# Padding ahead of the first fetch, two rows to a packet, and the first conversions spread over a mixture-of-experts stage

## The chip, the cores and the metric

The kernel runs on one core of one Trainium2 chip. The metric is device time in microseconds, the median of the runs shown. Beside these runs there is one profiled execution, whose trace is read below. Engines are named as the profile names them: PE (matmul), PEld (weight load), DVE, ACT, POOL, and SP, which issues nearly all DMAs; SPq is SP's instruction queue.

## The reference, cut to what matters

Three layers follow each other: a retention-like attention, a mixture of eight experts with sticky routing, and a Fourier mix with a two-layer channel network. Only the second is touched by the change:

```python
for b in range(B):                      # 4 sequences
    prev_e = -1
    for s in range(S):                  # 576 tokens each
        fresh_e = argmax(logits[b, s])
        e = fresh_e if s == 0 or local_gate[b, s] < 0.5 or prev_e < 0 else prev_e
        prev_e = e
        h = maximum(x[b, s] @ w1[e], 0)         # 512 -> 1024
        out[b, s] = p[e] * (h @ w2[e])          # 1024 -> 512
```

## The kernel before, in words

**Rows by expert.** At the end of the attention stage each token's row (512 values as a high and a low fp16 part, then its position and its gate: 1056 fp16, 2112 bytes) is scattered by POOL into a DRAM tensor `xs`, sorted by expert. The last six scatters go out just before the expert stage. Each expert gets a fixed number of rows (`CAPS`); what the routing doesn't fill is overwritten with zero rows: `pad(e)` (L1047) writes `CAPS[e] - 128` rows from an SBUF tile of zeros, `z`, 288 of them (608,256 bytes, 594 KB) for expert 1 and 160 or 192 for the others. Where they begin is a value that `tally` (L2019) computes on DVE and SP loads (`start(e)`). `fetch(e)` (L1012) then reads the expert's rows through two or one transposing DMAs into `xt`, and the positions and gates into `mt`. `fetch(0)` reads fixed places and waits for all scatters (`rows_in.before`); `fetch(1)` reads rows that `pad(1)` may have written, and waits for that. `apart` lifts the order between fetches and paddings of different experts; `Rows.add` lifts it between scatters. Neither lifts it between a padding and a scatter.

**Weights.** An expert's weights are eight pieces of 128x1024 fp32 (512 KB), 0 to 3 of w1 and 4 to 7 of w2. Each is sized (`absmax`, ACT L234), and for each four pieces a power of two is found: `peak` (DVE L250 to L255, makes `diag`), `spread` (one PE matmul L260 and a DVE reduction L261), `scale` (DVE L266, L269). Then `split` makes the high part (ACT L276) and the low part (DVE L281).

**Order.** The program's order on each engine is fixed by hand, an engine's instructions run in that order. A first batch of 256 rows of expert 0 (`weights(0)`, two tiles) begins in the attention stage. Then, for e = 0 to 7, a hidden stage of eight steps f (12 matmuls each into one PSUM bank out of four, then `relu`: ACT L826 and DVE L828, the latter frees the bank), and an output stage, a tile of 128 rows at a time (24 matmuls L840, ACT L852, a POOL scatter L854). `halves` (L931) deals other work to slots of these stages by numbers in `SLOTS`; stage n = 2e is the hidden stage of expert e, n = 2e + 1 its output stage. For expert 0 the work is written out in `moe` itself: `parts` splits expert 1's pieces 0 to 3, `sizes` sizes pieces 6 and 7 and begins the conversions.

**Conversions.** `Doubles` converts the channel network's weights, given as 64-bit doubles, to fp32 in 16 pieces, of which 14 go beside the experts: `load` (1 MB, tile `raw`, two buffers), `first` (DVE L294 to L298), `second` (DVE L303, L306), `absmax` (ACT), `store` (DMA).

The order on DVE after expert 0's hidden stage is `first(0)`, `peak` of expert 1's second half, `second(0)`, `first(1)`, `second(1)`, and then the reduction and scale of that second half, whose `spread` matmul PE has after step f = 0 of expert 1. On SP it is the weight loads 0 to 7 of expert 1, `fetch(0)`, `pad(1)`, `fetch(1)`, the loads of `raw` 0 and 1, and then weights of expert 2.

Of the kernel before, what the change touches and what calls it, by code (L numbers as in the profile page):

```python
# [10 lines left out]
FP16 = mybir.dt.float16  # L11
BF16 = mybir.dt.bfloat16
I32 = mybir.dt.int32
# [6 lines left out]
B, H, S, D = 4, 8, 576, 64  # L20
# [19 lines left out]
XW = 1056  # L40
NOPOS = 1 << 20
# [11 lines left out]
DONE = 14  # L53
# [774 lines left out]
    nc.vector.scalar_tensor_tensor(out=l[:, f, :], in0=ps, scalar=0.0, in1=h[:, f, :], op0=ALU.max, op1=ALU.subtract)  # L828


def outputs(nc, ps, q, x2, rows_out, w, hid, mt, fs, t, n, amid=None):

    h, l = w.dst
    k = 128 // min(128, n - 128 * t)
    r, d = 128 // k, 512 // k
    for f in range(8):
        for i, (m, x) in enumerate(((h, 0), (h, 1), (l, 0))):
            for j in range(k):
                c = 512 * (f % 2) + d * j
                nc.tensor.matmul(  # L840
                    out=ps[r * j : r * j + r, 0:d],
                    lhsT=hid[x][:, f, 128 * t : 128 * t + r],
                    rhs=m[:, 4 + f // 2, c : c + d],
                    start=(f == 0 and i == 0),
                    stop=(f == 7 and i == 2),
                )
        if f == 3 and amid:
            amid()

    def leave():  # L850
        y = q()[:, 0:d]
        nc.scalar.activation(out=y, in_=ps[:, 0:d], func=ACTF.Copy, scale=fs)  # L852
        rows_out.add(
            nc.gpsimd.indirect_dma_start(  # L854
                out=x2[:, :].rearrange("t (k d) -> (t k) d", k=k),
                out_offset=bass.IndirectOffsetOnAxis(ap=mt, axis=0),
                in_=y,
                in_offset=None,
                bounds_check=k * NT - 1,
                oob_is_err=False,  # L860
            )
        )

    return leave


class Late:
# [22 lines left out]
    def outputs(self, bank):  # L890
# [13 lines left out]
        second=0,  # L904
        spread=-1,
        split=(0.1, 1.1, 2.1, 3.1),
        raw=1.2,
        store=1.3,
        fetch=1.4,
# [7 lines left out]
        first=(0, 4.2),  # L917
        factors=0.2,
        split=(0.5, 0.6, 1.5, 2.7),
        second=2.8,  # L920
        load=(2, 3, 4, 5),
        size=(3.1, 4.1, 4.6, 5.2),
        raw=5.5,
        store=5.6,
# [6 lines left out]
def halves(weights, conv, n, slots, others=()):  # L931


    jobs = []

    def at(k, f, *a):
        jobs.append((k, len(jobs), partial(f, *a)))

    def matrix(m):
        return (weights(m // 2), m % 2) if m // 2 <= E else (None, 0)  # L940

    S = SLOTS[n % 2]
    if n <= DONE:
        at(S["own"], conv.absmax, n - 1)
    w, i = matrix(n + 1)
    if not (w.one and i):
        if n % 2 == 0:
            at(S["spread"], w.spread, i)
        at(S["spread"], w.scale, i)
    for p in range(4 if not w.one else EARLY_C1):  # L950
        at(S["split"][p], w.split, 4 * i + p)
    w, i = matrix(n + 2)
    if not w.one:
        for p in range(4):
            at(S["size"][p], w.absmax, 4 * i + p)
    if n % 2 or n == 2:
        for m, k in ((n + 3, "load"), (n + 4, "ahead"))[: 1 + n % 2]:
            w, i = matrix(m)
            if w and not (w.one and i):
                for p in range(4):  # L960
                    at(S[k][p], w.load, 4 * i + p)
    for k, f in others:
        at(S[k], *f)

    S = {**S, "first": (4, 0), "second": 5, "store": 5.1, "raw": 5.2} if n == 2 else S
    if n < DONE:
        if n % 2 or n == 2:
            at(S["first"][0], conv.first, n)
        at(S["second"], conv.second, n)
        at(S["store"], conv.store, n)  # L970
        if n + 2 < DONE:
            at(S["raw"], conv.load, n + 2)
        if n % 2 and n + 1 < DONE:
            at(S["first"][1], conv.first, n + 1)
    w, i = matrix(n + 2)
    if not (w.one and i):
        at(S["peak"], w.peak, i)
    todo = [[] for _ in range(slots)]
    for k, _, f in sorted(jobs, key=lambda x: x[:2]):
        todo[int(max(k, 0) * slots / 8)].append(f)  # L980
    return todo


def moe(octx, tc, nc, A, xs, x2, rows_in, rows_out, pieces, weights, who, conv, low, start, beyond, z, hid0, mt0, wst, small):
    ctx = ExitStack()
    pool = lambda **k: ctx.enter_context(tc.tile_pool(reuse_waits="tile", **k))
# [60 lines left out]
    def pad(e):  # L1047
        m = CAPS[e] - ZERO
        i = nc.sync.dma_start(
            out=xs[bass.ds(start(e), m), :].bitcast(I32).rearrange("(t p) c -> p t c", p=32),  # L1050
            in_=z[0:32].bitcast(I32).unsqueeze(1).to_broadcast([32, m // 32, XW // 2]),
        )
        apart(e, i)

# [9 lines left out]

        return fs, fill

    def out(w, hid, mt, fs, t, n, do, amid=None):
        y = lambda: wk.tile([128, 512], FP32, tag="y", name="y", bufs=3)
        ps = p2.tile([128, 512], FP32, tag="ps2", name="ps2")
        leave = outputs(nc, ps, y, x2, rows_out, w, hid, mt[:, t, 0:1], fs[:, t : t + 1], t, n, amid)  # L1070
        for job in do:
            job()
        leave()
# [3 lines left out]
    w1 = weights(1)  # L1077
    n = CAPS[8]
    pieces.more = more
    for p in range(4, 8):  # L1080
        w1.load(p)
    fetch(0)
    pad(1)
    fetch(1)
    conv.load(0)
    conv.load(1)
# [6 lines left out]
    def sizes():  # L1093
        for p in range(6, 8):
            w1.absmax(p)
        conv.first(0)
        w1.peak(1)
        conv.second(0)
        conv.store(0)
        conv.load(2)  # L1100
        conv.absmax(0)
        conv.first(1)
        conv.second(1)
        conv.store(1)
        conv.load(3)

    fs, fill = factors(weights(0), mt0, 2)
    fill()
    w1.peak(0)
    for t in range(2):  # L1110
        out(weights(0), hid0, mt0, fs, t, n, (parts,) if t else (), partial(w1.spread, 0) if t else None)

    v = weights(2)
    first = [[] for _ in range(8)]
    for p in range(4, 6):
        first[0].append(partial(w1.absmax, p))
    first[7].append(beyond)
    for f, p in zip((2, 3, 4, 5), range(4)):
        first[f].append(partial(v.load, p))
    for e in range(E):  # L1120
        w, n = weights(e), CAPS[e] if e < E - 1 else HEAD
        if e == E - 1:
            pieces.more = None
        xt, mt = X.pop(e)
        tiles = (n + 127) // 128

        todo = halves(weights, conv, 2 * e, 8, [("fetch", (fetch, e + 1))] if e + 1 < E else ()) if e else first
        hid = wk.tile([128, 2, 8, n], FP16, tag="hid", name="hid", padded_shape=[128, 2, 8, CAP])
        hid = [hid[:, x] for x in range(2)]
        for f in range(8):  # L1130
            if e == 0 and f % 4 == 0:
                four = [bank()[:, 0:n] for _ in range(4)]
                for part in (0, 2, 1):
                    for g in range(4):
                        products(nc, four[g], *w.dst, xt, f + g, (part,))
            if e == 0:
                ps = four[f % 4]
            else:
                ps = bank()[:, 0:n]
                products(nc, ps, *w.dst, xt, f)  # L1140
            for do in todo[f]:
                do()
            if f == 4 and e + 2 < E:
                pad(e + 2)
            for _ in relu(nc, ps, hid, f):
                pass
        fs, fill = factors(w, mt, tiles + (end.n + 127) // 128, small) if e == E - 1 else factors(w, mt, tiles)
        if e == E - 1:
            end.fs = fs

        def sides(mt=mt, tiles=tiles, n=n, e=e):
            for i, m in ((n // 128, n % 128), (tiles + end.n // 128, end.n % 128 if e == E - 1 else 0)):
                if m:

                    to, k = mt[:, i, 0:1], 128 // m
                    nc.vector.tensor_scalar(out=to, in0=to, scalar1=float(k), scalar2=side[k], op0=ALU.mult, op1=ALU.add)

        late = 0 < e < E - 1
        if not late:
            fill()  # L1160
            sides()
        if e == E - 1:
            mx.close()
            yield
        todo = halves(weights, conv, 2 * e + 1, tiles, [("factors", (f,)) for f in (fill, sides) if late]) if e else [[sizes]]
        for t in range(tiles):

            amid = partial(weights(e + 1).spread, 0, lambda: bank()[:, 0:128]) if e and t == 0 else None
            out(w, hid, mt, fs, t, n, todo[t], amid)
# [988 lines left out]
def fused_kernel(tc, A, out, stop=None):  # L2158
    nc = tc.nc
    with ExitStack() as ctx:  # L2160
# [5 lines left out]
        with tc.manual_schedule():  # L2166
# [39 lines left out]
            keep = ctx.enter_context(tc.tile_pool(name="keep", bufs=1))  # L2206
            fill = ExitStack()

            def zeros(pool):

                z = pool.tile([128, XW], FP16, name="z")
                nc.gpsimd.memset(z, 0.0)
                nc.gpsimd.memset(z[:, 1024:1026].bitcast(I32), NOPOS)
                return z

            z = zeros(fill.enter_context(tc.tile_pool(name="zp", bufs=1)))
# [64 lines left out]
            c2x = ExitStack()  # L2281
            cv = c2x.enter_context(tc.tile_pool(name="cv", bufs=1, reuse_waits="tile"))
            conv = Doubles(nc, cv, jobs)
            z = zeros(cv)
            steps = moe(ctx, tc, nc, A, xs, x2, rows_in, rows_out, pieces, weights, who, conv, low, start, beyond, z, hid0, mt0, wst, small)
            next(steps)
            for t, n in zip(tables, ("f_cs", "f_sn", "f_cd", "f_sd")):
# [53 lines left out]
```

## Time and profile before

| | |
|---|---|
| median of 3 runs | 803.86 us (801.23 to 806.83) |
| the profiled execution | 806.09 us, span of its trace 804.3 us |
| mean granted TensorE clock | 0.983 |
| PE busy | 738.5 us, 92% of the span |
| DVE busy | 590.8 us, 73% |
| ACT busy | 412.2 us, 51% |
| expert 0's first batch, output | PE from 124.8 us |
| expert 0's other rows, hidden and output | 135.2 to 150.5 us |
| expert 1, hidden and output | 150.5 to 193.1 us |
| expert 2 begins | 193.2 us |

The span leaves 1.8 us of the execution outside the trace. Busy shares are means over the whole kernel; what a stage waits for is read in rows of that stage.

### The profile page before, as it was taken

The page shows a single profiled execution, that of the slowest core. Times are in us where ns is not written, and L with a number is a line of the kernel's source. Part 1 is how long each engine was busy: PE and PEld are TensorE (multiplying, and loading weights), DVE is VectorE, ACT ScalarE, POOL GpSimd, SP SyncE. Part 2 cuts the span into 40 slices and gives each one's busy share as a digit, 9 for nine tenths or more (in the row PEclk, how much of TensorE's full clock was granted, in tenths as well). Part 3 has the DMA queues.
Part 4 walks back from the last instruction along what each step waited for, and adds up shares of the span by engine and source line. Part 5 has one row for each costly group of instructions (what it writes and reads, how often), then busy time and mean ns, then how long its engine had stood idle before and what let it go on. Part 6 is the DMA issues. An engine that isn't in the chain of part 4 may idle for free. (4 is left out here: it accounts for less than half of the span.)

```text
span 804.3 us, 17230 instructions
## 1 busy us (share of the span) xinstructions
PE 738.5 (92%) x6571; PEld 550.7 (68%) x6571; DVE 590.8 (73%) x1432; ACT 412.2 (51%) x829; POOL 129.3 (16%) x225
## 2 busy tenths in 40 slices
PE   8888898889999998889989998979899999999996
PEld 5777785545656555557635546868788888888885
DVE  3678886588889988857797984968968495737362
ACT  1356657278888797835728533515523361414140
POOL 3566443002102201113000111010010101010101
PEclk9999999899999999999999998999999999999999
DMA  9998348899999999850528266610370016110000
GB/s 292 360 317 297 118 139 277 274 318 379 261 338 324 259 314 326 271 174 29 167 93 313 93 197 170 189 58 2 106 206 2 27 53 172 53 40 15 27 2 27
DMA packets 91930, 142.29 MB, mean 177 GB/s; under 512 B 48116, under 2 KB 49017, under 8 KB 90814
## 3 DMA queue, kind: packets, MB, share of 16 engines
q1 hardware_dynamic: 87246, 126.78, 50.1%
q0 software_dynamic: 4592, 14.31, 4.7%
q8 instruction: 54, 0.88, 0.4%
q14 instruction: 38, 0.31, 0.1%
HBM read 97.55 MB, written 35.12 MB: 165 GB/s over the span
## 5 line engine op out<-in xcount | busy, mean ns | idle before, releaser
L1637 PE MATMUL g<-gxt,wh 128*128 128x256 f16 (+1 forms) x992 | 145.0, 287 | 4.5 <-DMA gxt<-un 4.3
L1951 PEld LDWEIGHTS <-hd 128*128 128x128 f16 x1176 | 114.9, 98 | 27.1 <-issue 7.6
L1637 PEld LDWEIGHTS <-wh 128*128 128x128 f16 x1056 | 103.9, 99 | 30.9 <-issue 8.4
L281 DVE SCALAR_TENSOR_TENSOR wl<-wst,ws,wh 128x1024 f16<-128x1024 f32 (+1 forms) x82 | 100.5, 1253 | 10.3 <-ACT wh L276 10.1
L276 ACT ACTIVATE wh<-wst,ws 128x1024 f16<-128x1024 f32 x80 | 89.1, 1140 | 24.6 <-DVE ws L269 24.6
L810 PE MATMUL ps<-xt,wh 128*128 128x320 f16 (+4 forms) x544 | 79.1, 284 | 11.1 <-DVE hid L828 7.6
L810 PEld LDWEIGHTS <-wh 128*128 128x128 f16 x640 | 57.6, 101 | 42.0 <-issue 24.4
L840 PE MATMUL ps<-wh,hid 128*128 128x512 f16 (+2 forms) x528 | 84.6, 302 | 0.2 <-ACT hid L826 0.2
L1951 PE MATMUL g<-wh,hd 128*128 128x256 f16 x448 | 79.7, 276 | 3.8 <-DVE u L1980 2.0
L1811 POOL DMA_INDIRECT out<-u,orow x18 | 19.3, 1075 | 394.1 <-DVE u L1980 296.9
L1637 PE MATMUL g<-gxt,wl 128*128 128x256 f16 (+1 forms) x496 | 81.0, 287 | 0.0
L1922 DVE SCALAR_TENSOR_TENSOR s<-g,r 128x256 f32<-128x256 f32 x168 | 53.3, 374 | 34.3 <-ACT hd L1916 33.6
L840 PEld LDWEIGHTS <-hid 128*128 128x128 f16 (+2 forms) x792 | 46.5, 100 | 42.9 <-issue 3.3
L234 ACT ACTIVATE wh<-wst 128x1024 bf16<-128x1024 f32 x66 | 69.3, 1050 | 6.4 <-DVE wst L306 4.1
L1980 DVE SCALAR_TENSOR_TENSOR u<-g,ffs,u 128x256 f32<-128x256 f32 (+1 forms) x63 | 34.1, 568 | 50.5 <-PE g L1951 49.8
L1915 ACT ACTIVATE r<-g 128x256 f32<-128x256 f32 x56 | 21.2, 378 | 95.8 <-PE g L1637 89.7
L1895 ACT ACTIVATE hd<-s 128x640 f16<-128x640 f32 x56 | 41.3, 737 | 47.1 <-DVE s L1922 47.1
L1951 PE MATMUL g<-e,hd 128*128 128x256 f16 x504 | 59.9, 273 | 5.2 <-DVE u L1980 4.2
L854 POOL DMA_INDIRECT x<-y,mt x25 | 32.2, 1287 | 198.8 <-ACT y L852 174.9
L1951 PE MATMUL g<-wl,hd 128*128 128x256 f16 x224 | 61.7, 276 | 0.0
L1637 PEld LDWEIGHTS <-wl 128*128 128x128 f16 x528 | 52.3, 99 | 12.3 <-issue 1.1
L840 PE MATMUL ps<-wl,hid 128*128 128x512 f16 (+2 forms) x264 | 56.3, 301 | 0.0
(302 smaller groups left out, 1293.9 us busy)
## 6 DMA issues: line engine op xcount, KB each, us to landing
wst<-in_moe_w SPq DMA_DIRECT2D x64, 512.0 KB
raw<-in_ch SPq DMA_DIRECT2D x14, 1024.0 KB
qk<-in_qkv SPq DMA_DIRECT2D x18, 512.0 KB
vk<-in_qkv SPq DMA_DIRECT2D x16, 512.0 KB
pair<-ch SPq DMA_DIRECT2D x32, 256.0 KB
ch<-d SPq DMA_DIRECT2D x14, 512.0 KB
wst<-ch SPq DMA_DIRECT2D x14, 512.0 KB
u<-u SPq DMA_DIRECT2D x9, 512.0 KB
```

The source lines that it names most:

```text
L234: self.nc.scalar.activation(out=x, in_=t, func=ACTF.Abs, accum_out=self.am[:, j : j + 1])
L276: self.nc.scalar.activation(out=self.dst[0][:, j, :], in_=self.pieces[j], func=ACTF.Copy, scale=self.by(j))
L281: self.nc.vector.scalar_tensor_tensor(out=l[:, j, c], in0=self.pieces[j][:, c], scalar=self.by(j), in1=h[:, j, c], op0=ALU.mult, op1=ALU.s ...
L810: nc.tensor.matmul(out=ps, lhsT=m[:, k, 128 * f : 128 * f + 128], rhs=xt[:, x + k, :], start=(k == 0 and i == 0), stop=(k == 3 and i == last),
L840: nc.tensor.matmul(out=ps[r * j : r * j + r, 0:d], lhsT=hid[x][:, f, 128 * t : 128 * t + r], rhs=m[:, 4 + f // 2, c : c + d], start=(f == ...
L854: nc.gpsimd.indirect_dma_start(out=x2[:, :].rearrange("t (k d) -> (t k) d", k=k), out_offset=bass.IndirectOffsetOnAxis(ap=mt, axis=0), in_ ...
L1637: nc.tensor.matmul(out=ps, lhsT=m[:, k + 4 * (f // 8), 128 * (f % 8) : 128 * (f % 8) + 128], rhs=xt[x][:, k, :], start=(k == 0 and i == 0) ...
L1895: nc.scalar.activation(out=hd[:, 0, 2:7], in_=s, func=ACTF.Copy, scale=C2 / 2)
L1915: nc.scalar.activation(out=r, in_=p[:, 1:3], func=ACTF.Relu)
L1922: V.scalar_tensor_tensor(out=d, in0=x, scalar=0.0, in1=y, op0=ALU.max, op1=op)
L1951: nc.tensor.matmul(out=ps, lhsT=hid[k][:, y, x, :], rhs=E[w][m][k], start=(k == 0 and m == y == 0), stop=(k == 7 and y == 1),)
L1980: V.scalar_tensor_tensor(out=y, in0=p, scalar=fs[:, c : c + 1], in1=y, op0=ALU.mult, op1=ALU.add)
```

## The change

1. `pad(1)` goes from behind `fetch(0)` to between the loads of pieces 6 and 7 of expert 1.
2. A padding writes two rows to a packet: `z` holds two rows per partition, and 16 partitions are read instead of 32. The memset that fills `z` is twice as wide, with two small ones behind it instead of one.
3. The `spread` of expert 1's first half comes after step 0 instead of step 3 of the first batch's second tile.
4. In expert 0's hidden stage the sizing of pieces 4 and 5 goes from step 0 to steps 4 and 5, and steps 4 to 7 run as those of other experts instead of in a batch of four.
5. `second(1)`, `store(1)` and the load of `raw` 3 go from `sizes` to slot 3 of expert 1's hidden stage, the conversion's `absmax(1)` to slot 4; `first(2)` from slot 4 to slot 5. `second(2)`, `store(2)` and the load of `raw` 4 go to the start of expert 1's output stage, `absmax(2)` to its second tile. `fetch(2)` goes from slot 1 to slot 3.

```diff
-        if f == 3 and amid:
+        if f == at and amid:
...
     S = SLOTS[n % 2]
-    if n <= DONE:
+    if n == 2:
+        S = {**S, "fetch": 3.6}
+    if 3 < n <= DONE:
         at(S["own"], conv.absmax, n - 1)
...
-    S = {**S, "first": (4, 0), "second": 5, "store": 5.1, "raw": 5.2} if n == 2 else S
-    if n < DONE:
-        if n % 2 or n == 2:
+    def ends(k, j):
+        at(k, conv.second, j)
+        at(k, conv.store, j)
+        if j + 2 < DONE:
+            at(k, conv.load, j + 2)
+
+    if n == 2:
+        ends(3, 1)
+        at(4.5, conv.absmax, 1)
+        at(5, conv.first, 2)
+    elif n < DONE:
+        if n == 3:
+            ends(0, 2)
+            at(2, conv.absmax, 2)
+        if n % 2:
             at(S["first"][0], conv.first, n)
...
-            out=xs[bass.ds(start(e), m), :].bitcast(I32).rearrange("(t p) c -> p t c", p=32),
-            in_=z[0:32].bitcast(I32).unsqueeze(1).to_broadcast([32, m // 32, XW // 2]),
+            out=xs[bass.ds(start(e), m), :].bitcast(I32).rearrange("(t p a) c -> p t (a c)", p=16, a=2),
+            in_=z[0:16].bitcast(I32).unsqueeze(1).to_broadcast([16, m // 32, XW]),
...
-    for p in range(4, 8):
+    for p in range(4, 7):
         w1.load(p)
+    pad(1)
+    w1.load(7)
     fetch(0)
-    pad(1)
     fetch(1)
...
         conv.first(1)
-        conv.second(1)
-        conv.store(1)
-        conv.load(3)
...
-        out(weights(0), hid0, mt0, fs, t, n, (parts,) if t else (), partial(w1.spread, 0) if t else None)
+        out(weights(0), hid0, mt0, fs, t, n, (parts,) if t else (), partial(w1.spread, 0) if t else None, 0)
...
-        first[0].append(partial(w1.absmax, p))
+        first[p].append(partial(w1.absmax, p))
...
-            if e == 0 and f % 4 == 0:
+            if e == 0 and f == 0:
...
-            def zeros(pool):
+            def zeros(pool, rows=1):
-                z = pool.tile([128, XW], FP16, name="z")
+                z = pool.tile([128, rows * XW], FP16, name="z")
                 nc.gpsimd.memset(z, 0.0)
-                nc.gpsimd.memset(z[:, 1024:1026].bitcast(I32), NOPOS)
+                for r in range(rows):
+                    nc.gpsimd.memset(z[:, r * XW + 1024 : r * XW + 1026].bitcast(I32), NOPOS)
...
-            z = zeros(cv)
+            z = zeros(cv, 2)
```

## Rows read from the trace of the kernel before

**Rows 1.** Waits of PE, 120 to 380 us: total us, times, longest.

```profile
PE peak L260 <- DVE diag L255: 9.3, 6, 3.1
PE ps L810 <- DVE hid L828: 7.6, 5, 3.1
```

**Rows 2.** Timeline of PE: start, us, engine, line, operation, count, [idle before <- releaser].

```profile
141.06 2.79 PE L810 MATMUL ps<-xt,wh 128*128 128x128 f16 x32 [3.00 <-DVE hid L828]
...
155.95 0.27 PE L260 MATMUL peak<-diag,onesb 128*128 128x128 bf16 x1 [3.14 <-DVE diag L255]
...
167.05 0.86 PE L810 MATMUL ps<-xt,wh 128*128 128x416 f16 x4 [3.06 <-DVE hid L828]
...
178.68 0.22 PE L260 MATMUL ps<-diag,onesb 128*128 128x128 bf16 x1 [0.44 <-DVE diag L255]
```

**Rows 3.** Timeline of DVE, expert 0's output stage to expert 2.

```profile
153.17 0.69 DVE L294 TENSOR_SCALAR d<-raw 128x1024 int32<-128x1024 int32 x1 [5.24 <-DMA raw<-in_ch]
...
155.61 0.29 DVE L255 TENSOR_SCALAR diag<-idn,wm 128x128 bf16<-128x128 f32 x1
...
161.67 1.23 DVE L306 SCALAR_TENSOR_TENSOR d<-raw,d 128x1024 int32<-128x1024 int32 x1
162.81 0.28 DVE L261 TENSOR_REDUCE wg<-peak 128x1 f32<-128x128 f32 x1
...
166.41 0.58 DVE L828 SCALAR_TENSOR_TENSOR hid<-ps,hid 128x416 f16<-128x416 f32 x1
...
195.13 0.29 DVE L261 TENSOR_REDUCE wg<-peak 128x1 f32<-128x128 f32 x1 [2.59 <-PE peak L260]
```

**Rows 4.** Timeline of ACT: the sizing of conversion 1.

```profile
162.99 1.06 ACT L234 ACTIVATE ab<-d 128x1024 bf16<-128x1024 f32 x1 [2.89 <-DVE d L306]
```

**Rows 5.** Timeline of SP's queue.

```profile
130.84 3.13 SPq L1019 DMA_TRANSPOSE xt<-xs  x2
...
135.55 0.39 SPq L1049 DMA_DIRECT2D xs<-z  x1
140.13 3.81 SPq L1019 DMA_TRANSPOSE xt<-xs  x1
...
147.78 0.85 SPq L322 DMA_DIRECT2D raw<-in_ch  x2
...
166.86 6.42 SPq L1019 DMA_TRANSPOSE xt<-xs  x1
```

**Rows 6.** Waits of SP's queue, 110 to 200 us.

```profile
SPq L1019 <- DMA xs<-xr,c_slot_i: 3.7, 1, 3.7
SPq L1019 <- DMA xs<-z: 3.4, 1, 3.4
```

**Rows 7.** Windows: us, busy of each engine, granted clock, DMA share, GB/s.

```profile
126.50:131.20 4.70, 4.70 (x23) 2.14 (x22) 3.40 (x15) 2.75 (x7) 0.00 (x0) 1.00 1.04 407
131.50:134.80 3.30, 3.30 (x18) 1.53 (x17) 0.69 (x4) 1.26 (x2) 0.99 (x2) 1.00 0.86 162
136.40:139.40 3.00, 1.66 (x30) 1.54 (x28) 3.00 (x3) 3.00 (x6) 0.74 (x1) 1.00 0.97 203
141.06:145.35 4.29, 4.29 (x48) 4.29 (x48) 1.12 (x5) 0.79 (x4) 0.00 (x0) 0.60 1.08 217
244.00:246.00 2.00, 2.00 (x34) 1.74 (x34) 1.97 (x3) 2.00 (x5) 0.00 (x0) 1.00 1.00 208
```

**Rows 8.** Timeline of POOL: the memset of z.

```profile
125.33 0.98 POOL L2212 MEMSET z<- 128x1056 f16 x1
```

**Rows 9.** Waits of DVE, 156 to 340 us, the whole answer.

```profile
DVE hid L828 <- ACT hid L826: 6.5, 11, 0.9
DVE wg L261 <- PE ps L260: 4.8, 5, 1.0
DVE wg L261 <- PE peak L260: 4.1, 6, 2.6
DVE wl L281 <- ACT wh L276: 3.2, 3, 1.7
```

More of the change, by code (lines that the diff above doesn't have):

```diff
@@ L828, in relu, with outputs @@
     nc.vector.scalar_tensor_tensor(out=l[:, f, :], in0=ps, scalar=0.0, in1=h[:, f, :], op0=ALU.max, op1=ALU.subtract)
-def outputs(nc, ps, q, x2, rows_out, w, hid, mt, fs, t, n, amid=None):
+def outputs(nc, ps, q, x2, rows_out, w, hid, mt, fs, t, n, amid=None, at=3):
     h, l = w.dst
@@ L1065, in factors, with out @@
         return fs, fill
-    def out(w, hid, mt, fs, t, n, do, amid=None):
+    def out(w, hid, mt, fs, t, n, do, amid=None, at=3):
         y = lambda: wk.tile([128, 512], FP32, tag="y", name="y", bufs=3)
         ps = p2.tile([128, 512], FP32, tag="ps2", name="ps2")
-        leave = outputs(nc, ps, y, x2, rows_out, w, hid, mt[:, t, 0:1], fs[:, t : t + 1], t, n, amid)
+        leave = outputs(nc, ps, y, x2, rows_out, w, hid, mt[:, t, 0:1], fs[:, t : t + 1], t, n, amid, at)
         for job in do:
@@ L1135, in moe @@
                         products(nc, four[g], *w.dst, xt, f + g, (part,))
-            if e == 0:
-                ps = four[f % 4]
+            if e == 0 and f < 4:
+                ps = four[f]
             else:
```

## The prediction

> **What bounds the kernel now.** I read the page first: PE is busy for 92% of the span, so time can only be saved where PE stands still. The change touches 120 to 195 us, so I then read who PE waits for [rows 1]: 9.3 us on a `diag` and 7.6 us on the relu that frees a bank, all on DVE. The timeline places the large ones [rows 2]: 3.00 us before the second half of expert 0's hidden stage, 3.14 us at the `spread` of expert 1's second half (155.95), 3.06 us before step 4 of expert 1 (167.05), and 0.44 us at 178.68. From 178.68 to expert 3 there is no wait of weight, so what counts is by how much PE's work at 178.68 comes earlier.
>
> The second wait is the gate. DVE's timeline shows why `diag` is late [rows 3]: DVE stands idle 5.24 us until the first `raw` lands, at 153.17, because `first(0)` stands ahead of `peak`. `raw` is late because of SP [rows 5]: it is issued at 147.78, behind `fetch(1)` (140.13), which waited for the padding issued at 135.55, itself behind `fetch(0)`, which waited for the last scatters until 130.84. SP's waits say the same [rows 6]: 3.7 us for the scatters, 3.4 us for `xs<-z`. PE finishes step 0 of expert 1 3.14 us before that chain is through. So whatever PE gains ahead of this point only lengthens its wait there. That prices two parts at once: the earlier `spread` (three steps of 0.65 us later by now) and the rearranged hidden stage of expert 0 (at most its wait of 3.00 us) are worth nothing while the chain of `raw` stands behind them. If `raw` came 3.1 us earlier or more, they would be the cover that lets PE profit.
>
> **The conversions' order.** This is a gain that does not depend on the padding. DVE has `second(1)` between the `spread` and its reduction now: L303 and L306 at 160.39 to 162.9, and the reduction follows at 162.81 [rows 3]. From the reduction to the relu that lets PE go on at 167.05 it is 4.2 us, whatever stands before. Without `second(1)` the reduction comes 2.4 us earlier (2 x 1.23 less the overlap of two instructions); and ACT no longer has the sizing of conversion 1 ahead of the first high part [rows 4], 0.5 us. So step 4 could begin 2.9 us earlier, at 164.15; PE's wait was 3.06, so PE is just ready. But `second(1)` comes back at step 3: DVE then has three low parts and three relus (about 1.2 + 0.5 us each, 5.1 us from 162.3), `second(1)` 2.4, a low part and the relu of step 3, and is at 171.6 us. Step 7 needs that relu; PE would be there at 170.5. So 1.1 us is given back, and step 7 begins at 171.6 instead of 173.4: 1.8 us gained. The 0.44 us at 178.68 goes too, since DVE has the same work up to there and lost no time: 2.2 us. `second(2)` moves into the output stage of expert 1, which has 2.4 us more DVE work then; DVE had 2.59 us of idle time at its end at 195.13 [rows 3], so at most some 0.2 us shows. **Sum of this part: 2.0 us gained.**
>
> What moves along on SP: `store(1)`, the load of `raw` 3 and `fetch(2)` now stand behind `second(1)`, so `fetch(2)` goes from 166.86 [rows 5] to some 170 us. It takes 6.42 us and is wanted at 193; nothing waits. The load of `raw` 4 is issued some 2 us later and first used some 2.4 us later. The absmaxes moved on ACT (1.04 us each) stay within its idle time.
>
> **The padding.** Now the order of flow is loads, `fetch(0)`, padding, `fetch(1)`. The windows show the parts [rows 7]: loads and scatters flow at 407 GB/s until 131.2, `fetch(0)` takes from 131.5 to 134.8 (3.3 us), the padding flows alone from 136.4 to 139.4 (3.0 us x 203 GB/s = its 608 KB). It costs 135.55 to 140.13 = 4.6 us on SP. If the padding were free, `fetch(1)` could go at 135.55, and `raw` and all behind it 4.6 us earlier. It is not free: its 608 KB then flow ahead of `fetch(0)`, in the same queue, with the 512 KB of load 7 (1.3 us at 407 GB/s). So `fetch(1)` goes at (begin of the padding's flow) + (its length) + 1.3 + 3.3 + 0.75 (134.8 to 135.55).
>
> *Begin.* A row doesn't show whether the padding must wait for the scatters. If not, it waits for the memset of `z` (0.98 us at 125.33, twice as long then [rows 8]), about 127.4, and its flow begins when the other loads are through, 131.2 - 1.3 = 129.9. If it must (the code lifts that order nowhere), it is issued at 130.84 and flows from 131.7 (0.85 us from issue to flow, as at 135.55 and 136.4); load 7 is then no longer ahead of the last scatters, which may bring both up to 1.3 us forward. I take the second.
>
> *Length.* Bounds are 1.5 us (407 GB/s, the rate of the loads) and 6.0 us. With all DMA engines busy (share 0.97) the padding gets 203 GB/s, and a later one alone gets 208 [rows 7], where loads into 128 partitions get 407. Either each of its rows is dear, and half as many packets take less; or reading `z` from 32 partitions limits it, and 16 partitions halve the rate. Scattered rows of the same 2112 bytes flow beside the loads in the 407 GB/s without pulling it down, so a packet of that size isn't what is dear. I take the second: 6.0 us. [...]
>
> *Sum.* `fetch(1)` at 129.9 + 6.0 + 5.35 = 141.25 without the wait for scatters, 143.05 with it, 141.75 if the scatters land 1.3 us earlier; against 140.13 that is 1.1, 2.9 and 1.6 us later, not earlier. `raw`, `diag` and PE's gate follow one to one. [...] With the 2.0 us: **0.9 us gained, 0.9 us lost, 0.4 us gained.** I take the last, 0.4 us. The sum is a difference of the profiled execution (806.09 us, 804.3 in the span, 2.2 us above the median); set against the median it is 803.86 - 0.4 = 803.5 us. Its own range is 0.9 us either way of no change, 803.0 to 804.8.
>
> **Smaller costs.** The longer memset: DVE and PE don't read `z`; at most 1 us on DVE if the two hinder each other, ahead of the gate and covered by it. Later paddings would take 4 us instead of 2; behind them no engine of [rows 9] waits for a DMA from 156 to 340 us, and `fetch(e)` there is ready long before it is used: nothing. Load 7 lands some 7 us later; its sizing is at 148: nothing.
>
> **The rivals.**
>
> *A. The packets were dear.* The padding flows in 1.5 to 3.0 us. For: half as many packets for the same bytes. Against: the scatters' rows above. `fetch(1)` then goes at 136.75 (129.9, 1.5 us) to 140.05 (131.7, 3.0 us), 3.4 to 0.1 us earlier. With 2.0: 2.1 to 5.4 us gained, 798.5 to 801.8.
>
> *B. No queueing.* The padding and load 7 flow beside the scatters before `fetch(0)` is ready, which keeps its place: `fetch(1)` at 135.55. For: SP is idle from 127 to 130.84. Against: the DMA engines are not (share 1.04 [rows 7]). 4.6 + 2.0 = 6.6 us gained, 797.3.
>
> *C. Slower: the padding behind the scatters, at half rate.* Place: SP's queue and the DMA engines, 131 to 143 us. The break-even is a `fetch(1)` at 142.13, which from 130.84 means a padding that flows longer than 5.1 us (120 GB/s). At 6.0 us and no earlier scatters it is 2.9 - 2.0 = 0.9 us slower; with 1 us more, for the clock's loss when the gate doesn't cover it, 1.9: 804.8 to 805.8.
>
> *D. The reorder does nothing*, because DVE, nearly full to 178 us, is the limit in any order: the 2.0 us are missing, 805.5 with my padding. Against: DVE is idle 1.7 us for the first high part and 5.24 us before.
>
> **How the numbers follow.** Chances: forecast 0.50, A 0.24, B 0.09, C 0.13, D 0.04. The range reaches from B to C: 797.5 to 806.0, which leaves out about 2 in 10 with the spread of medians (runs differ by 5.6 us). 1% is 8 us, about what a measurement of this kernel can tell from no change. Faster by that needs B and more: 0.06. Slower by it needs a chain that no row shows: 0.03. Same: 0.91.
>
> **What would show it.** In the changed trace: the padding's window, its GB/s (near 100 or above 200) and where it starts (127 or 131); a new wait of PE for `xt` of expert 0 at 135; `fetch(1)` on SP at 141 to 143 (or 136 to 140); the `spread` of expert 1 on PE 3.5 us behind the landing of `raw`; the wait before step 4 gone and about 1 us before step 7. I am wrong if `fetch(1)` is issued before 139, or if PE's gain at 178.68 differs from the shift of `raw` plus 2.

## The result, and the profile after

| | median, us | ratio to before (95%) |
|---|---|---|
| before, in the same comparison | 806.67 (801.23 to 808.36, 8 runs) | |
| with the change | 813.32 (808.99 to 816.77, 8 runs) | 1.009 (1.0065 to 1.0116) |

The forecast was 803.5 us in a range of 797.5 to 806.0, 0.4 us under the median of before that was then known (803.86); the change made the kernel slower by 0.9%, about 7 us. The profiled execution took 812.92 us, with a span of 811.1 and a clock of 0.978.

The waits of PE, 120 to 380 us, that answer to [rows 1] (line numbers are some 15 higher than before):

```profile
PE ps L810 <- DMA xt<-xs: 13.2, 3, 6.2
PE peak L260 <- DVE diag L255: 6.1, 4, 3.3
PE ps L810 <- DVE hid L828: 4.1, 6, 1.0
```

The two groups of before fell from 9.3 and 7.6 us to 6.1 and 4.1. A third stands above them that before did not have: PE waits three times for the rows of an expert. The timeline of PE has them, with one late `diag`:

```profile
143.53 3.57 PE L810 MATMUL ps<-xt,wh 128*128 128x128 f16 x32 [6.15 <-DMA xt<-xs]
...
172.89 0.86 PE L810 MATMUL ps<-xt,wh 128*128 128x416 f16 x4 [0.98 <-DVE hid L828]
...
197.29 0.23 PE L260 MATMUL peak<-diag,onesb 128*128 128x128 bf16 x1 [3.30 <-DVE diag L255]
...
278.98 0.65 PE L810 MATMUL ps<-xt,wh 128*128 128x288 f16 x4 [2.09 <-DMA xt<-xs]
...
309.94 1.12 PE L810 MATMUL ps<-xt,wh 128*128 128x288 f16 x4 [4.99 <-DMA xt<-xs]
```

The first belongs to expert 0, the last two to experts 5 and 6. Windows behind these last two (us; busy of PE, PEld, DVE, ACT, POOL; granted clock, DMA share, GB/s):

```profile
278.98:283.00 4.02, 4.02 (x34) 3.23 (x34) 2.63 (x7) 1.53 (x3) 0.86 (x2) 1.00 0.77 127
309.94:313.00 3.06, 3.06 (x14) 1.94 (x14) 0.00 (x0) 0.00 (x0) 0.00 (x0) 0.50 0.72 79
```

After the stop of 2.09 us PE ran on at a granted clock of 1.00, after that of 4.99 us at 0.50. So the wait at expert 6 costs more than its own length.

No row at expert 1's second `spread` has a wait; before it was 3.14 us [rows 2]. SP's queue, against [rows 5]: the padding, load 7, `fetch(0)`, `fetch(1)`, the raw pieces, the padding of expert 3 with raw 4 right behind it, and the fetches of experts 4 to 6:

```profile
132.34 0.39 SPq L1064 DMA_DIRECT2D xs<-z  x1
132.99 0.39 SPq L224 DMA_DIRECT2D wst<-in_moe_w  x1
133.66 7.29 SPq L1034 DMA_TRANSPOSE xt<-xs  x2
...
142.56 3.46 SPq L1034 DMA_TRANSPOSE xt<-xs  x1
...
149.13 0.85 SPq L322 DMA_DIRECT2D raw<-in_ch  x2
...
182.23 0.37 SPq L1064 DMA_DIRECT2D xs<-z  x1
...
183.70 2.71 SPq L322 DMA_DIRECT2D raw<-in_ch  x1
...
234.87 10.66 SPq L1034 DMA_TRANSPOSE xt<-xs  x1
...
264.43 11.14 SPq L1034 DMA_TRANSPOSE xt<-xs  x1
...
294.33 10.24 SPq L1034 DMA_TRANSPOSE xt<-xs  x1
```

And windows of the first padding and of the one of expert 3, with the same columns, against 203 and 208 GB/s in [rows 7]:

```profile
133.40:138.40 5.00, 3.97 (x19) 1.69 (x18) 3.79 (x5) 4.81 (x5) 0.80 (x2) 1.00 0.96 104
183.20:186.20 3.00, 3.00 (x16) 1.37 (x14) 2.96 (x6) 2.18 (x4) 1.21 (x2) 1.00 0.93 99
```

Both flow at half the rate of before, with nearly all DMA engines busy (shares of 0.96 and 0.93). To compare traces, in which the attention ahead of this stage ends up to 4 us apart, I count from the start of the first batch's output stage on PE (124.8 us before, 126.5 after). `spread`s are counted as PE runs them: the second is that of expert 1's second half, expert 5 starts between the ninth and the eleventh, expert 6 between the eleventh and the twelfth, and the fifteenth is the last of them. The last column is the issue of expert 6's rows on SP. Each number is a start in the timeline less that origin.

```
us from the origin       expert 0  2nd   3rd   4th   9th    11th   12th   15th   fetch(6)
before                     10.4    31.1  53.9  70.1  138.9  166.0  179.3  213.2   161.8
change                     17.0    31.7  51.1  70.8  139.7  169.0  186.3  220.5   167.8
r1 old paddings            14.4    28.6  48.8  65.1  133.9  161.0  175.2  209.3   159.5
r3 conversions alone       10.4    31.1  51.4  69.9  138.7  165.8  180.7  214.7   164.5
r6 first padding           17.8    32.1  51.9  68.2  137.0  164.0  177.4  212.8   161.2
r12 later paddings         14.3    29.8  49.2  68.5  138.8  168.1  187.5  221.5   167.5
r9 one row, 16             17.0    31.2  51.5  72.0  143.6  172.1  189.5  223.6   171.3
r5 two rows, 4 apart       14.3    29.8  50.1  66.5  135.4  165.1  182.9  217.3   165.0
r11 two rows, 7 apart      14.6    30.1  50.4  69.5  140.0  167.1  180.4  214.7   163.7
r8 one row, all over       13.6    28.2  48.5  64.8  133.7  160.8  174.1  208.7   158.6
r10 r8, raw 0 earlier      10.7    25.8  48.6  66.1  135.0  162.0  176.8  211.0   160.4
```

At the third `spread` the change is 2.8 us ahead of before; at the fourth this is gone, at the last it is 7.3 us behind, which is the 0.9%. Each row is one execution, and its total lies up to 4 us off the median of its kernel: r1's is 2.6 us and r6's 2.9 us under it, r3's 4.0 us and r5's 1.7 us over it. So small differences between two rows prove little, and the ratios below decide.

From the eleventh to the twelfth `spread` the change takes 17.3 us, of which 4.99 are the wait; r1 takes 14.2, of which 3.31 are its wait. The rest is 12.3 against 10.9 us: the first four matmuls behind the stop took 1.12 us in the change, at the granted clock of 0.50, and 0.65 in r1.

### The profile page after: what moved, and what is told of

It is laid out like the page before. It is cut to its first block, busy times and chain, and to the rows that moved or that the text cites. A ratio compares the mean times of both kernels' runs of the same rounds, so it can differ in the third digit from the quotient of the medians.

```text
span 811.1 us, 17229 instructions
## 1 busy us (share of the span) xinstructions
PE 741.1 (91%) x6571; PEld 552.4 (68%) x6571; DVE 590.9 (73%) x1432; ACT 411.8 (51%) x829; POOL 130.7 (16%) x226
## 5 line engine op out<-in xcount | busy, mean ns | idle before, releaser
L810 PE MATMUL ps<-xt,wh 128*128 128x320 f16 (+4 forms) x544 | 80.6, 287 | 20.6 <-DMA xt<-xs 13.2
L1964 PE MATMUL g<-e,hd 128*128 128x256 f16 x504 | 61.6, 277 | 5.9 <-DVE u L1993 4.9
```

Of the source, the lines that this page charges most:

```text
L810: nc.tensor.matmul(out=ps, lhsT=m[:, k, 128 * f : 128 * f + 128], rhs=xt[:, x + k, :], start=(k == 0 and i == 0), stop=(k == 3 and i == last),
L1964: nc.tensor.matmul(out=ps, lhsT=hid[k][:, y, x, :], rhs=E[w][m][k], start=(k == 0 and m == y == 0), stop=(k == 7 and y == 1),)
```

## The experiments

Ratios are to before, measured beside each; the interval is of 95%.

**r1: the change with the paddings as they were.**

```diff
-            out=xs[bass.ds(start(e), m), :].bitcast(I32).rearrange("(t p a) c -> p t (a c)", p=16, a=2),
-            in_=z[0:16].bitcast(I32).unsqueeze(1).to_broadcast([16, m // 32, XW]),
+            out=xs[bass.ds(start(e), m), :].bitcast(I32).rearrange("(t p) c -> p t c", p=32),
+            in_=z[0:32].bitcast(I32).unsqueeze(1).to_broadcast([32, m // 32, XW // 2]),
...
-            z = zeros(cv, 2)
+            z = zeros(cv)
```

With that the tile of zeros is one row wide again, and its memset is the old one; the same holds in r7 to r10.

> The change, with its paddings as before: single rows from 32 partitions. Theory P (reading 16 adjacent partitions halves a padding's rate; the longer flow makes the loss): padding 1 flows 3.0 us near 203 GB/s instead of 6, the wait of PE for xt of expert 0 shrinks from 6.2 to some 3 us, the new waits for xt of experts 5 and 6 (2.1 and 5.0 us) go, and the time is 0 to 3 us under the kernel before (ratio 0.996 to 1.000). Theory Q (the order on SP's queue: fetch(2) and a raw load behind second(1) put the queue behind, and it stays behind): the waits for xt of experts 5 and 6 remain, the ratio stays at 1.005 to 1.009.

0.9975 (0.9945 to 1.0005). The first padding flows at 204 GB/s; expert 0 waits 3.5 us for its rows, expert 5 not at all, expert 6 3.3:

```profile
132.90:135.40 2.50, 2.50 (x13) 1.13 (x12) 1.22 (x4) 2.06 (x2) 1.04 (x2) 1.00 1.00 204
```
```profile
140.63 2.72 PE L810 MATMUL ps<-xt,wh 128*128 128x128 f16 x32 [3.51 <-DMA xt<-xs]
...
299.97 0.65 PE L810 MATMUL ps<-xt,wh 128*128 128x288 f16 x4 [3.31 <-DMA xt<-xs]
```

So the new form of the paddings is the loss: 1.009 against 0.9975, and the intervals are apart.

**r2: the paddings alone on the kernel before**, the reverse edit.

> The kernel before with two-row packets from 16 partitions and nothing else of the change. Theory P: padding 1, still behind fetch(0), flows 6 us at 100 to 109 GB/s, fetch(1) is issued 3 us later (143 instead of 140), the gate 3 us later; the later paddings take 2 us more each and waits for xt of late experts appear; ratio 1.006 to 1.011. Theory Q: only the 3 us at the gate, no wait for xt later; ratio 1.002 to 1.004. If packets were dear and the rate not halved: padding 1 in 1.5 to 3 us, ratio 0.997 to 1.000.

1.016 (1.0133 to 1.0187). This run does not price the paddings. The build's scheduler also put SP's read of a count, which belongs to the overflow branch at 333 us, ahead of `fetch(1)`, and SP stood still for it (SP's waits: us in total, times, longest):

```profile
SPq L2106 <- DVE fs L1060: 10.0, 1, 10.0
```

The paddings are therefore priced on the change's own order, in r6 and r12, where SP's instructions are the same but for the paddings.

**r3: the conversions alone on the kernel before** (`halves` and `sizes` as in the change, the rest as before).

> The kernel before with the conversions moved (second(1), second(2), their stores, loads and sizings, first(2), fetch(2) to slot 3) and nothing else. Theory P: the wait before step 4 of expert 1 falls from 3.1 to under 0.7 us, about 1 us appears before step 7, no wait for xt; 1.5 to 2.5 us faster (ratio 0.997 to 0.998). Theory Q: fetch(2) some 4 to 6 us later on SP, the queue stays behind, waits for xt of experts 5 and 6 of 5 us or more; ratio 1.003 to 1.007.

0.9975 (0.995 to 1.0001). PE and DVE in its timelines:

```profile
195.92 0.23 PE L260 MATMUL peak<-diag,onesb 128*128 128x128 bf16 x1 [2.12 <-DVE diag L255]
...
305.30 0.65 PE L810 MATMUL ps<-xt,wh 128*128 128x288 f16 x4 [4.05 <-DMA xt<-xs]
```
```profile
193.13 0.69 DVE L294 TENSOR_SCALAR d<-raw 128x1024 int32<-128x1024 int32 x1 [2.10 <-DMA raw<-in_ch]
```

In before PE's wait at expert 6 was another:

```profile
304.09 0.22 PE L260 MATMUL peak<-diag,onesb 128*128 128x128 bf16 x1 [2.30 <-DVE diag L255]
```

2.5 us are gained at the third `spread` (51.4 for 53.9), and 2.3 of them lost at the fourth, because raw 4 lands late in this execution; expert 6 then waits 4.05 us for rows where before waited 2.30 us for `diag`. In the table it ends 1.5 us behind, in the medians level or a little ahead: no gain is shown.

**r4: paddings of one row from 96 partitions (80 for the smaller ones) on the kernel before.**

```diff
+        w = 80 if m % 96 else 96
-...rearrange("(t p) c -> p t c", p=32), in_=z[0:32]...to_broadcast([32, m // 32, XW // 2])
+...rearrange("(t p) c -> p t c", p=w), in_=z[0:w]...to_broadcast([w, m // w, XW // 2])
```

> The kernel before with paddings of single rows read from 96 partitions (80 where 96 does not divide) instead of 32. Theory P: padding 1 flows at 350 GB/s or more in 1.5 to 1.8 us instead of 3.0, fetch(1) is issued 1.2 to 1.5 us earlier (138.8), and the gate with it; ratio 0.996 to 0.999. If a row of 2112 bytes is what costs: the rate stays near 203 GB/s and the ratio at 1.000.

0.9992 (0.9976 to 1.0009). The first padding flows at 262 GB/s, not the 350 expected:

```profile
139.30:141.30 2.00, 1.45 (x26) 1.33 (x24) 2.00 (x3) 2.00 (x4) 0.00 (x0) 1.00 0.93 262
```

`fetch(1)` follows 4.34 us after it instead of 4.58, and the gate comes 0.2 us earlier. Faster paddings by themselves show no gain there; PE waits for no rows in that kernel.

**r5: two rows to a packet, source partitions 4 apart.**

```diff
-            in_=z[0:16].bitcast(I32)...
+            in_=z[0:64:4].bitcast(I32)...
```

> The change as it is, but the 16 source partitions of a padding lie 4 apart (0, 4, ..., 60) and not side by side; packets, their count and bytes are the same. Theory 'where the source lies': the half rate of the changed kernel (101 to 107 GB/s between 134 and 140 us) comes from 16 neighbouring partitions; spread over 64 it flows at about 203 GB/s as the old padding did, the two transposes of expert 0 take 5 us and not 7.3, and the ratio is that of the change with the old padding, 0.9975 (0.994 to 1.001). Rival 'the packet': two rows to a packet from 16 partitions are slow wherever they lie: still about 104 GB/s, ratio 1.009.

1.0014 (0.999 to 1.0039). Same packets, same number of partitions, and the flow is that of 32 neighbours:

```profile
134.90:137.40 2.50, 2.50 (x13) 1.09 (x12) 1.28 (x2) 2.32 (x3) 0.79 (x2) 1.00 0.92 201
```

So the half rate is a matter of where the source lies. But experts 5 and 6 still wait 2.02 and 5.51 us, and `fetch(6)` is 5.5 us later than in r1. Part of it is 1.5 us later at `fetch(2)` already; the rest is not explained. It is not the flow of its own later paddings: those of experts 3 to 7 take 1.8 to 2.7 us each from the first packet to the last, and 1.8 to 2.8 us in r1. A strided source took SP 0.67 us to issue here instead of 0.37, but so it did in r8 (0.73), without such waits.

**r6: the first padding alone in the new form; r12: the six later ones alone.** One condition chooses between the two forms, `e == 1` or `e != 1`.

> The change with two rows to a packet in the first padding (expert 1) alone; the six later ones in the old form, one row to a packet from 32 partitions. Theory 'the DMA engines are full to 345 us': the first padding costs its 2.6 us ahead of expert 0's rows and 3 us at expert 1's second spread, against the change with the old padding, and the later ones cost the rest: expert 5 starts without a wait for its rows, and the ratio is 1.001 (0.998 to 1.004). Rival 'all of it is lost at the first padding and only shifts': experts 5 and 6 wait 2 and 5 us as in the change, ratio 1.009.

> The change with the first padding (expert 1) in the old form and the six later ones as changed, two rows from 16 neighbours: the counterpart of the run with the first one alone (1.0006). Theory 'the later ones cost the larger share, through the one queue': the start is that of the change with the old padding (expert 0 at 14.4 us, second spread of expert 1 at 28.6), rows of experts 5 and 6 come late, or the fourth spread does; ratio 1.005 to 1.007. Rival 'the first padding costs nearly all': 0.9975 to 1.000.

1.0006 (0.9978 to 1.0035) and 1.0053 (1.003 to 1.0076). Against r1 that is 0.0031 and 0.0078; with r1's 0.9975 they add up to 1.0084, the change's 1.009. PE's waits, first r6 (6.9 us for the rows of expert 0, then almost none), then r12, with its fourth `spread`:

```profile
144.37 3.34 PE L810 MATMUL ps<-xt,wh 128*128 128x128 f16 x32 [6.92 <-DMA xt<-xs]
...
300.87 0.65 PE L810 MATMUL ps<-xt,wh 128*128 128x288 f16 x4 [0.80 <-DMA xt<-xs]
```
```profile
139.79 3.57 PE L810 MATMUL ps<-xt,wh 128*128 128x128 f16 x32 [3.45 <-DMA xt<-xs]
...
193.99 0.29 PE L260 MATMUL peak<-diag,onesb 128*128 128x128 bf16 x1 [2.95 <-DVE diag L255]
...
277.26 0.65 PE L810 MATMUL ps<-xt,wh 128*128 128x288 f16 x4 [2.29 <-DMA xt<-xs]
...
310.14 1.12 PE L810 MATMUL ps<-xt,wh 128*128 128x288 f16 x4 [7.09 <-DMA xt<-xs]
```

By these ratios some 2.5 us are the first padding's and 6 us the later ones'. The intervals of r6 and r1 overlap, so the first one's share is not clear of noise; those of r12 and r1 do not.

**r7: old paddings, the later six issued twice** (a loop of two around the DMA).

> The change with all paddings in the old form (one row to a packet, 32 partitions), but the six later ones issued twice, same rows, same zeros: their engine time doubles as in the changed kernel, the packets stay the old ones. Theory 'the DMA engines are full, and time on them is what counts': the start is as in the change with the old padding (expert 0 at 14.4 us from the first batch's output), then experts 5 and 6 wait for their rows as in the change (2 and 5 us or so); ratio about 1.005 (1.002 to 1.008). Rival 'it is something in the packets themselves' (or the engines have slack): no wait at expert 5, ratio 0.9975.

1.0211 (1.0173 to 1.025), far beyond either. The second copy writes the rows of the first, so SP waited until the first had landed, and everything behind with it:

```profile
SPq L1065 <- DMA xs<-z: 11.6, 2, 8.8
```

It priced that wait and not the bytes; r9 does what it was meant for.

**r8: one row to a packet, 32 partitions 4 apart over the whole memory.**

```diff
-            in_=z[0:32].bitcast(I32)...       (as in r1)
+            in_=z[0:128:4].bitcast(I32)...
```

> The change with one row to a packet again, from 32 partitions that lie 4 apart over all 128 (0, 4, ..., 124). Theory 'where the source lies': the rate grows once more, to 300 to 400 GB/s; the first padding takes 1.5 to 2 us and not 3, expert 0 starts 1 us or more before its 14.4 us in the change with the old padding, the later paddings take 5 to 8 us less on the full engines, so the wait at expert 6 (3.3 us there) shrinks; ratio 0.994 (0.990 to 0.998). Rival 'the writing side or the row bounds it at 203 GB/s': ratio 0.9975 and the same waits.

0.9939 (0.991 to 0.9968), faster than before; the interval overlaps with r1's. The flow of the first padding, and the two waits for rows that are left:

```profile
133.60:135.10 1.50, 1.50 (x8) 0.69 (x7) 0.48 (x1) 1.50 (x2) 0.45 (x2) 1.00 0.93 337
```
```profile
139.98 3.12 PE L810 MATMUL ps<-xt,wh 128*128 128x128 f16 x32 [2.75 <-DMA xt<-xs]
...
298.03 0.65 PE L810 MATMUL ps<-xt,wh 128*128 128x288 f16 x4 [1.47 <-DMA xt<-xs]
```

**r9: one row to a packet from 16 neighbours**, r1 with 16 for 32.

> The change with one row to a packet again (twice as many packets as the changed kernel), but read from the same 16 neighbouring partitions. Theory 'where the source lies, and time on the one queue is what costs': the paddings flow at 101 to 107 GB/s as in the changed kernel; expert 0 waits about 6 us for its rows, expert 5 about 2 and expert 6 about 5; ratio 1.009 (1.006 to 1.013). Rival 'two rows to a packet are slow, or hold up the loads behind them': the flow is about 203 GB/s, as with one row from 32 partitions, no wait at expert 5, ratio 0.9975.

1.010 (1.0073 to 1.0127), the change's own loss, with the old packets:

```profile
133.30:138.30 5.00, 4.14 (x20) 1.75 (x18) 3.75 (x5) 4.64 (x5) 0.96 (x2) 1.00 0.93 100
```
```profile
198.59 0.29 PE L260 MATMUL peak<-diag,onesb 128*128 128x128 bf16 x1 [4.14 <-DVE diag L255]
...
313.39 1.01 PE L810 MATMUL ps<-xt,wh 128*128 128x288 f16 x4 [5.25 <-DMA xt<-xs]
```

Only the wait at expert 5 failed to come; the time was lost at the fourth `spread` instead, for raw 4, and behind it four matmuls of PE took 1.27 us (198.67) where four of the same kind had taken 0.71 (193.20).

**r10: r8 with `fetch(0)` ahead of the padding again and the first raw piece ahead of `fetch(1)`.**

```diff
-    for p in range(4, 7):
+    for p in range(4, 8):
         w1.load(p)
-    pad(1)
-    w1.load(7)
     fetch(0)
+    pad(1)
+    conv.load(0)
     fetch(1)
-    conv.load(0)
     conv.load(1)
```

> One row to a packet from 32 partitions over all 128, as in the run that was 0.9939, with SP's order at the start: expert 0's rows, padding of expert 1, the first raw piece, expert 1's rows, the second raw piece. Theory 'the first raw piece sets expert 1's second spread, and expert 0 need not wait for the padding': expert 0 starts at about 10.4 us from the first batch's output (13.6 in that run) without a wait for its rows, the first raw piece lands some 5 us earlier, the spread stands at 24.5 to 26 us (28.2), and of these 2 to 3.5 us some stay to the end: ratio 0.990 to 0.993. Rival 'the one queue is the bound from there on': the start gains as said, but the rows of expert 6 are issued no earlier than 158.6 us from that point, PE waits 3 to 5 us there (1.5), and the ratio stays at 0.994.

0.9932 (0.9906 to 0.9958), not to be told from r8. The start went as foreseen (expert 0 at 10.7, the second `spread` at 25.8, 2.4 us ahead of r8), and these 2.4 us were gone at the third:

```profile
152.47 0.86 PE L810 MATMUL ps<-xt,wh 128*128 128x416 f16 x4 [2.01 <-DMA xt<-xs]
165.06 1.54 PE L810 MATMUL ps<-xt,wh 128*128 128x416 f16 x4 [3.93 <-DVE hid L828]
...
303.49 0.65 PE L810 MATMUL ps<-xt,wh 128*128 128x288 f16 x4 [3.24 <-DMA xt<-xs]
```

Expert 1's rows now come late, then a relu, and expert 6's rows are issued at 160.4, no earlier than r8's 158.6: the rival's picture.

**r11: two rows to a packet, partitions 7 apart** (`z[0:112:7]`).

> The change as it is, two rows to a packet from 16 partitions, but 7 apart (0, 7, ..., 105), so that they reach both halves of the memory. Theory 'only where the source lies counts': the flow is 250 to 350 GB/s, the paddings are done as soon as with one row from 32 partitions over all 128 (0.9939), and so is the rest: ratio 0.994 to 0.998, no wait at expert 5. Rival 'two rows to a packet also cost something of their own, as the 4-apart run suggests (203 GB/s at the start and yet 1.0014, with 2.0 and 5.5 us of waits at experts 5 and 6)': the start is as good, but experts 5 and 6 wait 2 and 4 us or more; ratio 1.000 to 1.002.

0.9959 (0.9935 to 0.9983), no wait at expert 5. The first padding flows at:

```profile
133.40:134.90 1.50, 1.50 (x9) 0.69 (x7) 0.59 (x1) 1.50 (x2) 0.33 (x2) 1.00 0.85 293
```

This is the change with nothing altered but which 16 partitions are read. So two rows to a packet need not cost anything. In this one execution raw 4 still came 2.7 us late at the fourth `spread`, which r8's did not.

## Why the prediction was wrong

**The step that failed** is in "Smaller costs": "Later paddings would take 4 us instead of 2; behind them no engine of [rows 9] waits for a DMA from 156 to 340 us, and `fetch(e)` there is ready long before it is used: nothing." The 4 us were right (99 GB/s in the window of 183 us). "Nothing" was wrong, and the trace of before held the reason in rows that the prediction does not use. The windows of before from 157 to 320 us:

```profile
157.00:200.00 43.00, 39.49 (x302) 21.50 (x301) 37.47 (x59) 31.55 (x51) 6.80 (x10) 0.98 0.98 349
...
230.00:260.00 30.00, 29.14 (x215) 18.54 (x214) 26.53 (x45) 25.82 (x46) 4.44 (x6) 1.00 0.97 311
260.00:290.00 30.00, 28.63 (x213) 18.31 (x212) 25.94 (x48) 25.73 (x46) 4.53 (x6) 1.00 0.95 306
290.00:320.00 30.00, 27.40 (x259) 16.77 (x258) 26.02 (x47) 24.03 (x41) 4.43 (x6) 1.00 0.92 292
```

The DMA engines are busy 92 to 98% of the time in these windows. PE, DVE and ACT wait for no transfer there ([rows 9] lists DVE's waits alone), but hardly any DMA time is free either. The fetches of before on SP, and where PE starts experts 5 and 6:

```profile
228.04 10.99 SPq L1019 DMA_TRANSPOSE xt<-xs  x1
256.71 11.18 SPq L1019 DMA_TRANSPOSE xt<-xs  x1
286.62 10.31 SPq L1019 DMA_TRANSPOSE xt<-xs  x1
```
```profile
274.39 0.66 PE L810 MATMUL ps<-xt,wh 128*128 128x288 f16 x4
...
300.15 0.66 PE L810 MATMUL ps<-xt,wh 128*128 128x288 f16 x4
```

A fetch takes SP 10 to 11 us here, where it took 3.1 and 3.8 at 130 and 140 us [rows 5]. From one to the next it is 28.7 and 29.9 us, while PE needs 25.8 from expert 5 to 6. The trace's records of the landings tell how much was left: in before the rows of experts 5 and 6 were in at 269.9 and 299.0 us, 13.2 and 12.3 us after their issue, and PE started 4.5 and 1.2 us later. In the change they took 14.6 (264.43 to 278.98) and 15.6 us (294.33 to 309.94), and PE waited. "Ready long before it is used" holds at expert 2, whose rows are in 17 us ahead of PE, and is all but used up at expert 6.

How a later padding may get through the queue is told by the change against r1, which differ in the paddings alone. `fetch(2)` to `fetch(6)` come 2.3, 4.5, 7.0, 8.5 and 8.3 us later, counted from the origin (r1: 44.4, 72.7, 101.4, 129.4, 159.5; change: 46.7, 77.2, 108.4, 137.9, 167.8). The steps are 2.2, 2.5 and 1.5 us, then none. The paddings between them are 405, 405 and 338 KB; at 101 instead of 203 GB/s they take 2.0, 2.0 and 1.7 us more. So each seems to go whole onto what is queued behind it. That is read from the match of the sizes and not shown by itself: SP's issues there also wait for DVE and ACT, and from the fourth `spread` on DVE and PE are late in the change.

**The gate** was right in its mechanism. The padding waits for the scatters (it is issued 5.8 us from the origin, 10.8 before) and flows at 104 GB/s: the 608 KB take 5.8 us, 6.0 predicted. `fetch(1)` is issued at 16.1 us from the origin, 17.0 predicted, which is partly luck. The padding begins 1.1 us later than in the case that was taken, since the scatters came 0.2 us earlier and not 1.3; from there to `fetch(1)` it is 10.2 us and not 12.2, as `fetch(1)` (142.56) doesn't wait until the rows of `fetch(0)` are in (143.53). Nor did all behind it follow one to one: the raw pieces are issued 0.4 us earlier than before (22.6 against 23.0 us from the origin), and the second `spread` stands 0.6 us later (1.6 predicted). PE stood still 6.15 us for expert 0's rows, the new wait for `xt` that the prediction looks for, and the gate covered it but for about 1 us: in r1, r3 and before the `spread` comes 8.1 to 8.2 us after the raw pieces' issue, in the change 9.1, with no wait for `diag`. That the early `spread` and the rearranged expert 0 are worth nothing by themselves fits r1: there the raw pieces are issued 2.6 us earlier than before, and the gate comes 2.5 us earlier. Up to the third `spread` the change does better than the forecast of 0.4 us, with 2.8; the signs that the prediction set itself lie up to there and came out or nearly so, and none of them looks at a later padding.

**The length.** Of its two readings the prediction took the second, that 16 partitions instead of 32 halve the rate, and 16 neighbours do, with either packet: 104 GB/s in the change and 100 in r9, against 203 in before and 204 in r1 from 32 neighbours. But the number of partitions doesn't settle the rate: 16 that lie 4 apart gave 201 GB/s (r5) and 16 that lie 7 apart 293 (r11), 32 that lie 4 apart 337 (r8), and r4's 96 neighbours 262, less than the 16 of r11. What it is about their place that sets the rate is not shown. (The 208 GB/s that the prediction reads as a later padding alone [rows 7] are of a window that ends 1 us behind its last packet; 243.2 to 244.9 us give 202. Nothing hangs on it.)

**The conversions' order** was 2.0 us; r3 shows 2.5 at the third `spread`, with step 4's wait down to 0.20 us and step 7's at 0.99 (1.1 predicted). The term mis-sized is what moves along on SP: `fetch(2)` was to come 3 us later and came 5.0 (42.1 to 47.1 us), and "the load of `raw` 4 is issued some 2 us later and first used some 2.4 us later" was 4.9 us later (53.8 to 58.7). It sits behind that fetch; in r3 it lands late, and the fourth `spread` takes the gain back. In the change DVE waits for it too, 3.28 us, and PE 3.30:

```profile
194.51 0.69 DVE L294 TENSOR_SCALAR d<-raw 128x1024 int32<-128x1024 int32 x1 [3.28 <-DMA raw<-in_ch]
```

But there it is not the order alone. r1 and r6 have the same order and the old later paddings, and no wait at the fourth `spread`; the change, r9 and r12 have the slow ones and wait 3.30, 4.14 and 2.95 us. Raw 4 is issued right behind the padding of expert 3 (183.70 and 182.23 us), so the "nothing" of the later paddings seems to have failed here first, 12 us behind one of them. A slow padding is not needed for such a wait: r3, r10 and r11 have 2.12, 1.19 and 2.71 us.

**The rivals.** A and B are out: the packets were not dear, and the padding did wait. D is out, since r3 gained its 2.5 us at the third `spread`. C named the right part, "the padding behind the scatters, at half rate", but its place, "131 to 143 us", and with it its price, 0.9 to 1.9 us, were those of the first padding; r6 gives that one 2.5 us against r1, and the seven together cost 9 us (1.009 against 0.9975). No run shows the 1 us that C adds for the clock by itself: in the change the 32 matmuls behind the stop at expert 0 took 3.57 us at a granted clock of 0.50 (143.53 to 147.10 us), in before 2.79 us in a stretch at 0.60 ([rows 2] and [rows 7], 141.06).

**What stays open:** why r5, at 201 GB/s, loses 4 us more than r1 between `fetch(2)` and `fetch(6)`; how a later padding's time passes from transfer to transfer, which is read from the sizes alone; and whether the conversions' order alone gains anything in the median, as its interval ends at 1.0001.

## What to carry to other kernels

Before a transfer is priced at nothing, read the DMA share of the stretch in which it flows and not only who waits there: on a queue that is full (DMA shares of 0.92 to 0.98 in the windows of before), time that is added can come out at a transfer behind it, here at raw 4, 12 us behind a padding, and, as it adds up, at the rows of experts 5 and 6, about 100 us on. Ask for the slack of those transfers, from landing to use, expert by expert. And a source that is written out many times should lie spread over the partitions: the change with 16 partitions that lie 7 apart instead of the first 16 flows at 293 GB/s and not 104 and is at 0.9959 and not 1.009, and single rows from every fourth of the 128, at 337 GB/s, are at 0.9939.

## What the runs showed that was not expected

Speeding up the paddings gave less than slowing them down cost: at 262 GB/s the kernel before showed no gain (0.9992), and on the change's order 337 GB/s (r8) against 204 (r1) is 0.4% with overlapping intervals, while some 100 GB/s cost that order 1.2% against r1. A padding that names strided partitions took SP 0.67 us (r5) to 0.73 (r8, r10) to issue, one with neighbouring ones 0.37 to 0.38 (r12, r9; medians of seven paddings each).
